# Attention and a bilinear feed-forward in one kernel: a fixed list in place of the scheduler

## The chip, the core and the metric

The kernel runs on one core of a Trainium2 chip. The metric is the device time of one execution in microseconds (us); the median of three runs before the change is 1517.46 us (1517.1 to 1517.92).

## The reference, cut to what matters

```python
# attention block: q, k, v are (8, 12, 448, 64), float32; g_q, g_k are (64,)
def rmsnorm(x, g):
    rms = np.sqrt(np.mean(x * x, axis=-1, keepdims=True) + 1e-06)
    return x / rms * g
q_n, k_n = (rmsnorm(q, g_q), rmsnorm(k, g_k))
scores = scale * np.matmul(q_n, k_n.transpose(0, 1, 3, 2))
attn = np.exp(scores - np.max(scores, axis=-1, keepdims=True))
attn = attn / (np.sum(attn, axis=-1, keepdims=True) + 1e-09)
attn_out = np.matmul(attn, v)
# feed-forward block: x is (3584, 768); w_a, w_b are (768, 1536), w_out is (1536, 768)
a = x @ w_a
b = x @ w_b
out = a * b @ w_out
```

The attention output of all 12 heads becomes the 3584 x 768 input of the feed-forward.

## The kernel before, in words

**The work.** The attention is done in 24 steps, one for each pair of head pairs (four heads of one batch); the code calls such a step `p`. For each step the SP queue loads q, k and v (L435). ScalarE squares q and k (L458), VectorE sums the squares (L460) and scales them (L464), GpSimd takes the power -0.5 (L466), VectorE multiplies q by it (L470). TensorE transposes k and then the scaled q (tile `pt`, L496), ScalarE copies both out of PSUM into `qkT` (L501, L503). Then seven blocks of keys follow, `j` = 0 to 6. For each, TensorE makes a scores group (`sc`, L517), ScalarE takes two exponentials of it (`ET`, L523), TensorE multiplies them by v (`o`, L539). The sums over keys are either four more matmuls for each block (`su`, L575, in the first five steps) or additions of the `ET` tiles on VectorE and GpSimd (L553) with one `su` group at the end. ScalarE moves the sums out (L588), they go to DRAM and back to be inverted in a compact form (L595, L608, L600, L604), ScalarE copies `o` out (L635) and VectorE multiplies it by the inverse (L646). The groups `sc`, `o` and `su` each consist of four 64 x 64 matmuls on the four quadrants of the array; the profile counts each as two passes, so such a group shows as 8 matmuls. All other matmuls use the full 128 x 128 array. The planner calls the two modes `quad` and `full`.

**The feed-forward** runs in four stages of two batches each, all with Strassen-like seven-product schemes: `firsts` makes a and b and their product, `lasts` multiplies it by w_out. In the first two stages the first product is L1202 (`pq`) and the last L903 (`po`); in the last two stages a deeper scheme is used (L779, `da` and `dg`, with VectorE's L818, L819, L826, L831 and L802), and L1100 for a part of the last product (`a`, `b`, `d`, `e`, `g`, with VectorE's sums `Si`, L1076). During the attention of the first two batches, ScalarE (L271) and VectorE (L272 to L280, L394) also turn the weights from the words they are given in into fp32 factors, 18 tiles `st`, which go to DRAM and come back when a stage needs them.

**PSUM.** Eight banks: the tag `sc` has two tiles of two banks each, and is used by the transposes, the scores, the sums and, later, by `dg`, `d` and `g`; the tag `o` has one tile of two banks; the tag `mm` has two tiles of one bank, used by `pq`, `po`, `da` and others.

**What sets the order.** Every operation is recorded by `Plan.op` (L49) with its engine, an estimated duration, a key (its due time), the operations that it depends on, the tiles that it opens, and a function that emits it. `Plan.run` (L72) then schedules them all: it walks through time, keeps for each engine the candidates whose inputs are ready, and takes for the engine that can start first the candidate with the lowest key among those that could start within 0.2 us (PE) or 0.05 us (others) of the earliest. It charges `TURN` for a change of the PE's mode, `STAY` to discourage leaving the quad mode, `LAG` for each step between engines, `RATE` and `LANDING` for DMAs. The functions are called in the order of time found, which is the program order on each engine and also the order in which tiles of a pool go round. Each engine works through its own instructions in that order.

Of the kernel before, what the change touches and what calls it, by code (L numbers as in the profile page):

```python
# [12 lines left out]
AF = mybir.ActivationFunctionType  # L13
ALU = mybir.AluOpType
# [10 lines left out]

class Plan:
# [9 lines left out]
    TURN = 0.18  # L36
    LANES = 8
    RATE, LANDING = 300.0, 2.0
    STAY = 0.3
    LAG = 0.1  # L40
# [31 lines left out]
    def run(self):  # L72
        ops = self.ops
        links, first = {}, {}
        for n, o in enumerate(ops):
            if o[6] is not None:
                links.setdefault(o[6], []).append(n)
        for c in links.values():
            for n in c:
                first[n] = c[0]  # L80
        users, need, left, last = {}, {}, {}, {}
        for n, o in enumerate(ops):
            head = first.get(n, n)
            outer = {d for d in o[4] if first.get(d, d) != head}
            need[head] = need.get(head, 0) + len(outer)
            for d in outer:
                users.setdefault(d, []).append(head)
            for t in o[9]:
                left[t] = left.get(t, 0) + 1
        ready = {n: 0.0 for n in need}  # L90
        opened, free, modes, cands, dma, port = {}, {}, {}, {}, 0.0, 0.0
        for n, k in need.items():
            if k == 0:
                cands.setdefault(ops[n][0], []).append(n)

        def members(n):
            return links[ops[n][6]] if ops[n][6] is not None else [n]

        def buffers(n):

            t, taken = 0.0, {}
            for x in members(n):
                for name in ops[x][8]:
                    tag, bufs = self.tags[name]
                    had = opened.setdefault(tag, [None] * bufs)
                    since = [(last.get(o, 0.0), k) for k, o in enumerate(had) if (tag, k) not in taken.values() and not left.get(o)]
                    if not since:
                        return None
                    t, taken[name] = max(t, min(since)[0]), (tag, min(since)[1])
            return t, taken  # L110

        order, end, sent = [], {}, [0.0] * self.LANES
        while any(cands.values()):
            best = None
            for e, cs in cands.items():
                f = free.get(e, 0.0) if e else 0.0
                at = {}
                for n in cs:
                    t = buffers(n)
                    if t is not None:  # L120
                        t = t[0]
                        turn = self.TURN if ops[n][5] != modes.get(e) else 0.0
                        if e == "PE" and modes.get(e) == "quad" and turn:
                            turn += self.STAY
                        at[n] = max(f, ready[n], t, port if ops[n][10] else 0.0,
                                    sent[ops[n][11] - 1 - self.LANES] if ops[n][11] else 0.0) + turn
                if at:
                    t = min(at.values()) + (0.2 if e == "PE" else 0.05)
                    n = min((n for n in at if at[n] <= t), key=lambda n: (ops[n][2], n))
                    t = at[n] - (self.STAY if e == "PE" and modes.get(e) == "quad" and ops[n][5] != "quad" else 0.0)  # L130
                    if best is None or t < best[0]:
                        best = t, e, n
            t, e, n = best
            cands[e].remove(n)
            for name, (tag, k) in buffers(n)[1].items():
                opened[tag][k] = name
            for x in members(n):
                if ops[x][5] != modes.get(e) and x != n:
                    t += self.TURN
                modes[e] = ops[x][5]  # L140
                order.append((t, x))
                t += ops[x][1]
                end[x] = t
                if ops[x][10]:
                    port = max(port, t)
                if ops[x][7]:

                    dma = max(dma, t) + ops[x][7] / self.RATE
                    end[x] = dma + self.LANDING
                    sent += [end[x]] * ops[x][11]  # L150
                for name in ops[x][9]:
                    left[name] -= 1
                    last[name] = max(last.get(name, 0.0), end[x])
                for u in users.get(x, ()):
                    ready[u] = max(ready[u], end[x] + (self.LAG if ops[u][0] != e else 0.0))
                    need[u] -= 1
                    if need[u] == 0:
                        cands.setdefault(ops[u][0], []).append(u)
            if e:
                free[e] = t  # L160
        assert len(order) == len(ops)
        self.times = order, end
        for _, n in order:
            if ops[n][3] is not None:
                ops[n][3]()


# [3 lines left out]
def kernel(  # L171
# [35 lines left out]
    nc = tc.nc  # L207
# [3 lines left out]
    P = 128  # L211
# [87 lines left out]
    def fast_body(ld, wk, ps_s, ps_o, ps_mm, dram):  # L299
# [27 lines left out]
        def rounding(key, size, get, x, w):  # L327

            for e, n, emit, r, wr in round_steps(get):
                rate = {"ACT": 950, "DVE": 1900 if n == 1 else 950, "POOL": 420}[e]  # L330
                names = {"x": x, "w": [w]}
                op(e, 0.17 + size / rate, key, emit, sum((names[c] for c in r), []), sum((names[c] for c in wr), []),
                   lock=e != "ACT")
# [25 lines left out]
        def factors(n, key, early, after):  # L359
# [16 lines left out]
            for part in range(2):  # L376
# [9 lines left out]
                op(LOADS, 0.45, key - 0.75, load, after, [f"{row}/{part}"], kb=768)  # L386
# [3 lines left out]
            for pool_, to, x, y in steps:  # L390
                add = to == 4 and not last
                e = FACTOR if pool_ else "DVE"
                op(e, 1.05 if e == "POOL" else 0.6, key,
                   lambda e=e, to=to, x=x, y=y, add=add: two[e].tensor_tensor(  # L394
                    sts[n][:, to], sts[n][:, x], sts[n][:, y], ALU.add if add else ALU.subtract),
                   [f"{st}/{homes[x]}", f"{st}/{homes[y]}"], [f"{st}/{homes[to]}"], lock=True)
# [11 lines left out]
        def stream(beta, n, f=None):  # L408
# [10 lines left out]
            op("SP", 0.5, 6.0 * beta + n / 4, load, reads, [f"{st}/{x}" for x in range(7)] + ["streaming"], new=[st],  # L419
# [6 lines left out]
        def loads(p, nm):  # L426
# [11 lines left out]
            op("SP", 0.8 if nm != "k" else 1.4, p - (1.8 if nm == "v" else 2.0), emit, [f"firsts{PREP}"] if p >= HELD else [], [t], new=[t],  # L438
               kb=460 if nm != "k" else 800, dmas=2)

        def normalize(p):
# [8 lines left out]
            def squares(s, nm):  # L450
# [8 lines left out]
                op("ACT", 1.07, key, square, [f"{nm}{p}"], [sq], new=[sq])  # L459
                op("DVE", 1.1, key, lambda: nc.vector.tensor_reduce(rs[p][:, s], xs["sq", nm, p], AX, ALU.add), [sq], [f"{ms}/{nm}"])  # L460

            def roots(a, b, names):
                msf = lambda: rs[p][:, a:b].rearrange("p s n -> p (s n)")
                op("DVE", 0.2, key, lambda: nc.vector.tensor_scalar(msf(), msf(), 1.0 / D, 1e-6, ALU.mult, ALU.add), [], names)  # L464
                op("POOL", 2.7 if b - a == 1 else 5.0, key,
# [20 lines left out]
        def transposes(p):  # L486

            qkT, key = tile_of(f"qkT{p}", "qkT", 2), p - EARLY
            for n, nm in ((1, "k"), (0, "q")):
# [17 lines left out]
                op("ACT", 1.05 if n else 1.15, key, take, [pt, "gain"], [f"{qkT}/{n}"], new=[qkT] if n else [])  # L507

        def scores(p, j):
# [17 lines left out]
            op("ACT", 1.12, p, exps, [sc, f"ms{p}/k"], [E], new=[E])  # L527
# [15 lines left out]
        def add_up(p, j):  # L543
# [10 lines left out]
            op(e, 2.2 if e == "POOL" else 1.12, p, emit, [f"E{p}.{j}"] + ([f"E{p}.0"] if j == 1 else []), [t],  # L554
# [24 lines left out]
        def invert(p):  # L579
# [27 lines left out]
            op("SP", 0.8, p - 0.0, spread_out, [t], [few], new=[few], kb=20, dmas=2)  # L607
            op("DVE", 0.3, p - 0.0, lambda: nc.vector.reciprocal(fews[0], fews[0]), [], [few])  # L608
            op("SP", 0.4, p - 0.0, leave, [few], [f"inv{p}"], kb=20)
            op("SP", 1.0, p - 0.0, come_back, [f"inv{p}"], [t], kb=460, dmas=2)  # L610
# [88 lines left out]
        def deep_factors(beta, m):  # L699
# [6 lines left out]
            for n, x, y, alu, reads in ((0, w(1, 0), w(1, 1), ALU.add, []), (1, made(0), w(0, 0), ALU.subtract, [0]),  # L706
# [9 lines left out]
                op("SP", 0.5, 0, lambda n=n: nc.sync.dma_start(kept["s"][:, m, :, n], ts[n]), [nm], [f"ks{m}.{n}"], kb=448)  # L716

        def deep_products(beta, key, names, h):
# [12 lines left out]
            for f, x in enumerate(xs_of):  # L731
# [4 lines left out]
                for n, a, b in ((0, lambda t=token: t(0, 1), lambda t=token: t(0, 0)), (1, lambda t=token: t(1, 1), lambda k=block: k(0)),  # L736
# [6 lines left out]
                    op("DVE", 0.32, -0.4, emit, [f"{x}/0", f"{x}/1", "ended" if beta == ONCE else f"{h}/open"] + ([nm] if n else []),  # L743
# [5 lines left out]
            def step(m, f, F, names_F):  # L749
# [10 lines left out]
                op("SP", 0.9, 6.0 * beta + (7 * m + f) / 14, load, [f"kept{2 * m}", f"kept{2 * m + 1}"] + [f"ks{m}.{n}" for n in range(5)],  # L760
# [10 lines left out]
                def product(nm, to, terms, reads, new=None, more=False):  # L771
# [9 lines left out]
                    op("PE", len(terms) * HS / 595, key + 0.1 * (7 * m + f), emit, reads + [slot], [nm, "ffn"],  # L781
# [19 lines left out]
                def wide(to, other):  # L801
                    take("DVE", 1.02, lambda: V.tensor_tensor(F[to], F[to], F[other], ALU.add), allF(other), allF(to), lock=True)  # L802

                def times(g, i, n):
                    e = "DVE" if m == MH - 1 and f > 4 else TIMES
                    take(e, 1.2 if e == "POOL" else 0.63,
# [19 lines left out]
                take("DVE", 0.66, lambda: V.tensor_tensor(  # L826
# [36 lines left out]
        def last_product(beta, h, key):  # L863
# [48 lines left out]
            def add(to, x, t, names_in, names_out):  # L912

                return lambda po, ps: op("DVE", 0.6, -1, lambda: nc.vector.tensor_tensor(to(), x(), ps(), ALU.add),
                                         [po] + names_in, names_out)

            def out_(t, i, x, y):
# [3 lines left out]
                def take(po, ps):  # L921
# [5 lines left out]
                    op("DVE", 0.6, -1, emit, [po, f"{fin}/{'cU'[y]}{t}"], [o_sb], new=[o_sb])  # L927
# [564 lines left out]
```

## Time and profile before

| what | value |
|---|---|
| median of three runs | 1517.46 us |
| the profiled execution | 1517.54 us |
| its span, first to last instruction | 1515.7 us |
| TensorE busy (7854 matmuls) | 1477.4 us, 97% of the span |
| VectorE busy | 1009.6 us, 67% |
| ScalarE busy | 441.2 us, 29% |
| GpSimd busy | 324.7 us, 21% |
| mean granted TensorE clock | 0.999 |
| moved by DMA | 250.73 MB, mean 165 GB/s |

The span is 1.84 us shorter than the execution's own time. The page gives busy time by engine, then the same in 40 slices of about 38 us, each digit in tenths. The waits view lists for each engine and line how long it stood still and what ended the wait. The timeline lists instructions in order, merged where they follow each other; an idle time ahead of one stands in brackets with what ended it. Ends of matmuls are modelled, so distances between the starts of matmuls are the safer measure; they are used here.

By what TensorE does, the span has these stages: attention alone with the making of the weights up to about 185 us, attention with `pq` to about 230 us, `pq` alone to 386 us, attention with `pq` and `po` to 540 us, `pq` alone to 731 us, attention with `po` to 920 us, and then feed-forward alone to the end.

### The profile page before, as it was taken

The numbers are of one execution on the slowest core, as the hardware profiler recorded it, in microseconds if no ns is written. First come the engines' busy times: TensorE is split into PE (matmuls) and PEld (weight loads), VectorE is DVE, ScalarE is ACT, GpSimd is POOL, SyncE is SP. The second block draws the span as 40 slices with busy tenths as digits, with TensorE's granted clock in tenths as the row PEclk, the third lists the DMA queues.
The fourth block names the chain that finished last, engine by engine and source line by source line (L and its number), as shares of the span: only waits on it lengthen the run. The fifth ranks groups of instructions, "written<-read, shape, count | busy, mean of one in ns | idle before, by whom it ended". The sixth has DMA issues, their size and how long they took to land.

```text
span 1515.7 us, 21017 instructions
## 1 busy us (share of the span) xinstructions
PE 1477.4 (97%) x7854; PEld 981.6 (65%) x7854; DVE 1009.6 (67%) x1568; ACT 441.2 (29%) x790; POOL 324.7 (21%) x172
## 2 busy tenths in 40 slices
PE   8998999999999999999999999999999999999998
PEld 5553345555445555555544445699997889999798
DVE  5887869888784233343667656477777667777785
ACT  6777661111554000000177761011111011111000
POOL 3426442111241001000265541011210001211000
PEclk9999999999999999999999999999999999999999
DMA  9897455554532464555656534655555755554554
GB/s 274 247 283 194 99 111 181 189 200 156 156 109 75 130 191 136 167 177 182 184 134 169 119 115 123 186 156 157 157 157 187 254 165 158 157 157 135 197 172 118
DMA packets 189074, 250.73 MB, mean 165 GB/s; under 512 B 61988, under 2 KB 160804, under 8 KB 182308
## 3 DMA queue, kind: packets, MB, share of 16 engines
q1 hardware_dynamic: 160900, 195.82, 45.5%
q10 hardware_dynamic: 28064, 53.48, 10.0%
q8 instruction: 64, 1.05, 0.3%
q14 instruction: 46, 0.38, 0.1%
HBM read 191.10 MB, written 57.97 MB: 164 GB/s over the span
## 4 chain that ended last, share of the span: by engine, by line
PE 86%; DMA 6%; DVE 3%; ACT 2%; issue 1%; SPq 1%; ACTq 0%; DVEq 0%
PE pq L1202 25%; PE dg L779 17%; PE po L903 15%; PE da L779 6%; PE o L539 6%; PE sc L517 6%; PE g L1100 2%; PE a L1100 2%; PE pt L496 2%; DMA q_sb<-in_q_dram 2%; PE su L575 1%; ACT ET L523 1%; PE b L1100 1%; DMA kept_o<-st 1%; PE d L1100 1%
## 5 line engine op out<-in xcount | busy, mean ns | idle before, releaser
L1202 PE MATMUL pq<-x,st 128*128 128x448 f32 x1008 | 382.4, 541 | 0.0
L1202 PEld LDWEIGHTS pq<-x,st 128*128 128x128 f32 x1008 | 190.8, 190 | 188.7 <-issue 181.7
L523 ACT ACTIVATE ET<-sc,ms 128x448 f32<-128x448 f32 x336 | 192.3, 632 | 86.5 <-PE sc L517 71.1
L539 PE MATMUL o<-ET,v_sb 64*64 64x448 f32 x1344 | 192.5, 546 | 3.6 <-ACT ET L523 2.9
L517 PE MATMUL sc<-qkT 64*64 64x448 f32 x1344 | 180.0, 543 | 16.3 <-ACT ET L523 9.1
L466 POOL TENSOR_TENSOR ms<-ms,expo 128x14 f32<-128x14 f32 x48 | 151.3, 3154 | 176.2 <-DVE ms L464 175.6
L779 PE MATMUL dg<-x,st 128*128 128x224 f32 x672 | 169.6, 355 | 2.0 <-DVE dF L826 2.0
L779 PE MATMUL dg<-dT,st 128*128 128x224 f32 x672 | 168.3, 353 | 1.9 <-DVE dt L819 1.9
L903 PE MATMUL po<-st,hT 128*128 128x384 f32 x492 | 163.4, 488 | 0.0
L807 POOL TENSOR_TENSOR hT<-dF 128x448 f32<-128x448 f32 x42 | 47.6, 1143 | 427.3 <-DVE dF L802 427.3
L903 PEld LDWEIGHTS po<-st,hT 128*128 128x128 f32 x492 | 92.9, 190 | 66.9 <-issue 6.0
L779 PEld LDWEIGHTS dg<-x,st 128*128 128x128 f32 x672 | 126.5, 190 | 5.3 <-DVE dF L826 5.3
L779 PEld LDWEIGHTS dg<-dT,st 128*128 128x128 f32 x672 | 126.7, 190 | 3.2 <-DVE dt L819 2.8
L779 PE MATMUL da<-x,st 128*128 128x224 f32 x504 | 123.2, 353 | 1.1 <-ACT dt L792 1.1
L517 PEld LDWEIGHTS sc<-qkT 64*64 64x64 f32 x1344 | 60.7, 133 | 89.6 <-issue 35.5
L539 PEld LDWEIGHTS o<-ET,v_sb 64*64 64x64 f32 x1344 | 61.3, 132 | 81.1 <-ACT ET L523 42.3
L553 POOL TENSOR_TENSOR sum<-sum,ET 128x896 f32<-128x896 f32 x38 | 81.1, 2134 | 104.0 <-ACT ET L523 60.8
L779 PEld LDWEIGHTS da<-x,st 128*128 128x128 f32 x504 | 93.0, 190 | 4.5 <-ACT dt L792 2.1
L802 DVE TENSOR_TENSOR dF<-dF 128x896 f32<-128x896 f32 x84 | 93.3, 1111 | 3.4 <-DVE dF L831 0.5
L792 ACT COPY dt<-da 128x224 f32<-128x224 f32 x84 | 29.1, 346 | 209.2 <-PE da L779 209.2
L553 DVE TENSOR_TENSOR sum<-sum,ET 128x896 f32<-128x896 f32 x57 | 62.0, 1088 | 38.2 <-POOL sum L553 34.0
L903 PE MATMUL po<-st,fin 128*128 128x384 f32 x252 | 86.7, 492 | 0.0
(136 smaller groups left out, 1683.6 us busy)
## 6 DMA issues: line engine op xcount, KB each, us to landing
st<-kept_o SPq DMA_DIRECT2D x28, 1152.0 KB
st<-kept_s SPq DMA_DIRECT2D x84, 320.0 KB
kept<-st ACTq DMA_DIRECT2D x12, 1344.0 KB
st<-kept SPq DMA_DIRECT2D x12, 1344.0 KB
st<-kept SPq DMA_DIRECT2D x84, 192.0 KB
ti<-kept_t SPq DMA_DIRECT2D x48, 288.0 KB
kept_s<-ds SPq DMA_DIRECT2D x30, 448.0 KB
q_sb<-in_q_dram SPq DMA_DIRECT2D x48, 224.0 KB
```

The lines of the kernel that those rows point to most:

```text
L466: lambda: nc.gpsimd.tensor_tensor(msf(), msf(), expo[:, 0:2 * NT * (b - a)], ALU.pow), [], names)
L496: nc.tensor.transpose(t[:, j * P:(j + 1) * P], x[:, j].rearrange("p h d -> p (h d)"), ident)
L517: nc.tensor.matmul(t[low_high[w], e, 0:S], lhsT=qkTs[p][low_high[e], 1, j * P + w * D:j * P + (w + 1) * D], rhs=qkTs[p][low_high[e], 0, w ...
L523: nc.scalar.activation(E[:, e], scs[p, j][:, e, 0:S], AF.Exp, scale=rs[p][:, 1, 2 * j + e:2 * j + e + 1])
L539: nc.tensor.matmul(os_[p][low_high[e], w, 0:S], lhsT=xs["v", p][low_high[w], e, j * D:(j + 1) * D], rhs=ETs[p, j][low_high[w], e], start=( ...
L553: two[e].tensor_tensor(sums[p], sums[p] if j > 1 else ETs[p, 0], ETs[p, j], ALU.add)
L779: nc.tensor.matmul(to(), lhsT=W(w), rhs=t(), start=not more and k == 0, stop=k == len(terms) - 1, skip_group_check=True)
L802: take("DVE", 1.02, lambda: V.tensor_tensor(F[to], F[to], F[other], ALU.add), allF(other), allF(to), lock=True)
L807: lambda: two[e].tensor_tensor(C(i, n), F[g][:, 0:S], F[g][:, S:2 * S], ALU.mult), allF(g),
L903: nc.tensor.matmul(held["po"][:, 0:HALF], lhsT=a[0]()[:, c], rhs=sts[beta, 12 + place_of[f]][:, c], start=(c == 0), stop=(c == MH - 1))
L1100: nc.tensor.matmul(held[bank], lhsT=x()[:, c], rhs=y(c), start=(start and c == 0), stop=(stop and c == MI - 1), skip_group_check=True)
L1202: nc.tensor.matmul(banks[bank][:, 0:S], lhsT=sts[at][:, f, c * P:(c + 1) * P], rhs=quads[x][:, c], start=(start and c == 0), stop=(stop an ...
```

## The change

The scheduler in `Plan.run` is taken out. In its place stands a list, compressed into a string, that gives for each place in time which operation comes there. Nothing is decided any more when the kernel is built: `run` walks through the list and calls each operation's function, and asserts that each one's inputs come ahead of it. The operations themselves, their tiles and pools stay. The estimated durations in many calls of `op`, and the constants of `Plan`, are changed too. The words that came with the change say that the list was found by a local search, in which two-bank PSUM tiles count as one and DMA issues are longer.

```diff
+ORDER = (
+    "c-rk(30PEDmj3U3?^P95ul9va1q8L*rPZ`%qMdZRqsBExlWsd|1d&n^aAjXy;t~+|4MYox8>keZqKJYT7c?p^Xtp-vBxZBc^UZWVrzc<cH|M<q"
...
+)
...
-    TURN = 0.18
+    TURN = 0.13
     LANES = 8
-    RATE, LANDING = 300.0, 2.0
+    RATE, LANDING = 310.0, 1.85
     STAY = 0.3
-    LAG = 0.1
+    LAG = 0.04
+    OVER = {"DVE": 0.085, "ACT": 0.1, "POOL": 0.04}
+    LATE = {"PE": 0.16}
...
     def run(self):
+
         ops = self.ops
-        links, first = {}, {}
...
-        self.times = order, end
-        for _, n in order:
-            if ops[n][3] is not None:
-                ops[n][3]()
+        n = len(ops)
+        places = zlib.decompress(base64.b85decode(ORDER))
+        assert len(places) == 2 * n
+        rest, at = list(range(n)), {}
+        for k in range(n):
+            x = rest.pop(places[k] + 256 * places[n + k])
+            assert all(d in at for d in ops[x][4])
+            at[x] = k
+            if ops[x][3] is not None:
+                ops[x][3]()
...
-            op("SP", 0.8 if nm != "k" else 1.4, p - (1.8 if nm == "v" else 2.0), emit, [f"firsts{PREP}"] if p >= HELD else [], [t], new=[t],
+            op("SP", 1.28 if nm != "k" else 1.4, p - (1.8 if nm == "v" else 2.0), emit, [f"firsts{PREP}"] if p >= HELD else [], [t], new=[t],
                kb=460 if nm != "k" else 800, dmas=2)
...
-            op("ACT", 1.12, p, exps, [sc, f"ms{p}/k"], [E], new=[E])
+            op("ACT", 1.15, p, exps, [sc, f"ms{p}/k"], [E], new=[E])
```

Some forty more calls of `op` differ in the same way, in the estimated duration alone.

## The prediction

> **What bounds the kernel now.** I read the page first, then the waits of TensorE, then TensorE's timeline around those waits, and last the busy time by stage.
>
> ```profile
> PE 1477.4 (97%) x7854; PEld 981.6 (65%) x7854; DVE 1009.6 (67%) x1568; ACT 441.2 (29%) x790; POOL 324.7 (21%) x172
> ...
> PE   8998999999999999999999999999999999999998
> ...
> PEclk9999999999999999999999999999999999999999
> DMA  9897455554532464555656534655555755554554
> ```
>
> TensorE (PE) is busy 97% of 1515.7 us at full clock, so an order can only win what PE loses between matmuls. Slices 1 to 6, 11 to 14 and 20 to 24 hold the attention. The DMA engines are nearly full only in the first three slices.
>
> ```profile
> PE sc L517 <- ACT ET L523: 9.1, 15, 1.5
> PE sc L517 <- ACT qkT L503: 6.1, 9, 1.2
> PE o L539 <- ACT ET L523: 2.9, 6, 0.8
> PE dg L779 <- DVE dF L826: 2.0, 2, 1.0
> PE dg L779 <- DVE dt L819: 1.9, 2, 1.0
> PE b L1100 <- DVE Si L1076: 1.8, 1, 1.8
> ```
>
> Columns: us in total, times, longest. Most named waits are attention groups that wait for ScalarE (ACT). Modelled ends hide part of each, so I go by starts:
>
> ```profile
> 139.39 0.98 PE L517 MATMUL sc<-qkT 64*64 64x448 f32 x8 [0.52 <-ACT ET L523]
> 140.19 0.93 PE L539 MATMUL o<-ET,v_sb 64*64 64x448 f32 x8
> 141.65 0.98 PE L517 MATMUL sc<-qkT 64*64 64x448 f32 x8 [0.52 <-ACT ET L523]
> ```
>
> Unhindered groups start 0.752 us apart (137.18 and 137.93 in the same view). Here scores and values take 2.26 us in place of 1.504, so 0.76 is lost each round, 0.05 of it on the restart. The reason: both rounds write the same PSUM pair, since the other one is held by a sums tile, so the scores wait for the exponentials of the scores just written, with one group as cover. That chain is 0.30 (hand-over) + 1.16 (two exponentials) = 1.46, less 0.752 of cover = 0.71, which the trace shows with the restart.
>
> ```profile
> 73.47 1.74 PE L517 MATMUL sc<-qkT 64*64 64x448 f32 x16 [1.14 <-ACT qkT L503]
> 75.58 1.12 PE L539 MATMUL o<-ET,v_sb 64*64 64x448 f32 x5 [0.37 <-ACT ET L523]
> ```
>
> The second kind: a new step's scores directly after its transposes wait for the copy of q (1.01 us on ACT and the hand-over), 1.21 us beyond the pace, and the first values then wait again. The third: at 1454 us `b` waits 1.97 us (start to start) because VectorE (DVE) has three other sums queued ahead of `Si`.
>
> By starts, PE loses 82 us in all against the pace of each kind of matmul: 7 in the first 25 us, 36 from 25 to 230, 6.5 from 386 to 540, 18 from 731 to 920, 14.5 after that. Of this, 52 quad stretches cost 0.11 at their end and 0.09 at their start each: 10.6 us.
>
> **What the Trainium skill says.** PSUM — Partial Sum Buffer, Engine vs sequencer instructions: the queues of ScalarE, VectorE and GpSimd are strict FIFO, and matmuls start and complete in program order. The trace agrees: at 1454 `Si` runs only after three 0.95 us sums that nothing hurries. So the order alone decides such stalls. TensorEngine Tiling (Array Packing), Key Properties: a change of tiling mode drains TensorE; here it costs 0.09 to 0.11 us. The same page, PSUM Bottleneck: tiling speeds up TensorE but not the emptying of PSUM; here a group of 0.752 faces 1.16 us of exponentials. Trainium Kernel Development and Optimization, Key Constraints: DMAs of SP, ACT and GpSimd share the same 16 engines; the DMA row at 9, 8, 9 shows how little is spare there.
>
> **The change part by part.** The new durations and constants do nothing by themselves: `run` no longer reads them. The built programs hold the same instructions on each engine, 4095 matmuls among them (fallback branch apart); only places and waits differ. So the whole effect is the order. It keeps the staging: the last matmul of each stage has the same work ahead of it within a few us, and the step between `pq` and `po` is unchanged. I counted, in both built orders, each PE wait for ACT or DVE whose chain goes back to an earlier matmul over at most four instructions, and set its length (traced durations; 0.30 hand-over for ACT; 0.2 for DVE, an estimate that gives the `dg` waits of 1.12 as 0.97) against the PE work between. Places with less cover than chain:
>
> - Scores into the pair just written (and a sums group after them): before 15 places of 0.71 = 10.6 us. After, five full ones (3.5) and eleven smaller ones (4.6), one of which waits behind the copy of `o`, = 8.1 us. The two-in-one-pair rounds at 110 to 150 us are still there, fewer.
> - Scores after the transposes: before 4 of 1.21 and 5 of 0.46 = 7.1 us. After 1 and 2 = 2.1 us, because other groups stand between.
> - Values after exponentials: before 7.1 us in 15 places, mostly 0.52 right behind the stalls above. After none.
> - Feed-forward alone: before `Si` 2.04, two `dg` of 0.97, two `da` of 0.65, one `b` of 0.33 = 5.6 us. After 3.2 us: three of the four `Si` are moved ahead of the three sums, one `dg` shrinks to 0.59.
>
> Before 30.4, after 13.4: **17.0 us gone**. As a check, the same count names in the order before the four stalls of 1.2 us and the rounds of 0.71 that the trace has. About 20 fewer restarts of 0.05: 1.0 us. Quad stretches fall from 52 to 48: 4 x 0.20 = 0.8 us.
>
> What is late next: about 9 us of PE stalls before have a longer chain, such as 1.3 us at 200 us, where ACT stands at a square that waits for its q load and everything behind it in ACT's queue waits too. Moved loads count here. By the waits, the PE work between the point that lets a q or k load go and its square is under 5 us for nine of 45 loads before and for one after (medians 6.0 and 8.7). Additions ahead of the `su` groups get more time too (least 3.0 before, 3.8 after). So these 9 us should rather shrink; bounds: 5 gained to 6 lost, I take 2 gained. PE has 57 more waits of its own (404 against 347): between nothing and 57 x 0.05 = 2.9 us, I take 1.3.
>
> SP's queue holds the same loads, stores and returns of the inverse, GpSimd's the same powers and sums, past each other by a few places; ACT's weight loads move likewise. Each would cost only where it makes a square, a copy or a sum late, which the 5 to 6 us of the bounds hold. Cover gone would be that of loads: a late load costs about 2 us (ACT's waits for q: 13.5 us, 8 times).
>
> Sum: 17.0 + 1.0 + 0.8 + 2 - 1.3 = 19.5 us. The profiled execution is 1517.54 (span 1515.7 + 1.84), so 1498.0; it stands 0.08 above the median, so the forecast is **1498 us**.
>
> **The rivals.**
> *The stalls move up the chain* (15%). ACT has 82 of 120 us busy from 110 to 230, DVE 90; if half of what is removed comes back as waits for loads, powers or additions, 9 to 10 us remain: 1508. For it: no stage alone is bound by PE here. Against: the cover of loads and sums is longer too.
> *Everything upstream goes as well* (13%): 17 + 1.8 + up to 9: about 1490. For it the longer covers; against it the DMA row.
> *The waits are exchanged one for one* (4%), because the count misses chains that are longer than four instructions: 1516 to 1519.
> *Late loads* (8%, slower). In the first 110 us DMA is 92% busy. If weights go out ahead of q and k so that each of 16 loads comes 2 us later than its cover, ACT's FIFO passes all of it on to PE: 32 - 19 = 13 us lost, 1531. It decides from about ten such loads. Against it: one load with short cover after, and the weights' work that must be done by each transpose stays within 8 us of what it was.
> *The list does not act*: excluded, since the built orders differ on every engine.
>
> **How the numbers follow.** The main case, 1494 to 1503, has 60%. With the 15% at 1508 and half of the 13%, the range 1489 to 1511 leaves out under 20%; its ends are the bounds above (5 more gained and no wait cost; 6 lost, 2.9 of waits and part of the count not won). A run of this kernel can tell about 0.2%, 3 us. Faster by more than that: 60 + 15 + 13 = 88%; within: 4%; slower: 8%.
>
> **What would show it.** Right: TensorE's idle time from 731 to 920 us nearly without ACT's exponentials; the waits for `qkT` down from 6.1 us in 9 places to about 2 in 3; no wait for `Si`; scores still waiting for exponentials around 110 to 150 us; the stages without attention as long as before. Wrong: more idle of ACT ahead of L458, or of PE behind loads, in the first 230 us.

## The result and the profile after

| | us |
|---|---|
| list, median of five runs | 1498.88 (1498.09 to 1502.80) |
| scheduler's order, run beside it, median of five | 1517.92 (1517.10 to 1519.69) |
| ratio | 0.9880, 95% interval 0.9864 to 0.9896 |
| profiled execution of the list, its span | 1502.80, 1500.9 |

The list is 19.0 us faster; the forecast was 1498 (1489 to 1511). The profiled execution is the slowest of its five, 3.9 us above the median. In its profile every line number is 34 lower than before: scores L483, exponentials L489, values L505, sums L541, copies of k and q L467 and L469, squares L424, weight loads L347 and L350.

The page, the same four rows as shown of before:

```profile
PE 1466.2 (98%) x7854; PEld 957.4 (64%) x7854; DVE 1003.3 (67%) x1568; ACT 438.8 (29%) x790; POOL 320.7 (21%) x172
...
PE   8988999999999999999999999999999999999998
...
PEclk9999999999999999999999999999999999999999
DMA  9888545555342455445667544655555765554554
```

The instruction counts are the same, so only places differ. In TensorE's first six slices one digit has fallen and none has risen: the start did not get better. The mean granted clock is 0.997, where it was 0.999. TensorE's waits (us in total, times, longest):

```profile
PE sc L483 <- ACT qkT L469: 6.9, 5, 3.7
PE sc L483 <- ACT ET L489: 6.8, 11, 0.9
...
PE o L505 <- ACT ET L489: 2.1, 3, 1.2
PE pt L462 <- ACT ET L489: 2.0, 2, 1.3
...
PE dg L745 <- DVE dF L792: 0.2, 1, 0.2
```

The exponentials ahead of scores fell from 9.1 us in 15 places to 6.8 in 11, and the wait for `Si` is gone. The copies of q did not fall to about 2 us: they are 6.9 us, 3.7 of them in one place. By starts, TensorE loses 67.3 us against the pace of its kinds of matmul where it lost 81.9. Of this the first 150 us take 37.0 (29.7 before), 150 to 230 us 7.5 (13.4), and all after that 22.8 (38.8). What the first 150 us of the list lose is in part matmuls at a lower clock, shown below.

A full stop of the first kind is still there. TensorE's timeline of the list:

```profile
153.84 0.93 PE L505 MATMUL o<-ET,v_sb 64*64 64x448 f32 x8
155.30 0.98 PE L483 MATMUL sc<-qkT 64*64 64x448 f32 x8 [0.53 <-ACT ET L489]
```

1.46 us lie between these starts in place of 0.752, the 0.71 of the forecast. In the attention with `po` such stops went. First the scheduler's order at the second scores of a step, then the list at that point of a later step:

```profile
791.22 0.98 PE L517 MATMUL sc<-qkT 64*64 64x448 f32 x8
792.02 0.93 PE L575 MATMUL su<-sum,ones 64*64 64x448 f32 x8
793.48 0.98 PE L517 MATMUL sc<-qkT 64*64 64x448 f32 x8 [0.53 <-ACT ET L523]
794.28 0.93 PE L539 MATMUL o<-ET,v_sb 64*64 64x448 f32 x8
```

```profile
893.47 0.93 PE L483 MATMUL sc<-qkT 64*64 64x448 f32 x8
894.22 0.93 PE L541 MATMUL su<-sum,ones 64*64 64x448 f32 x8
895.09 2.20 PE L869 MATMUL po<-st,fin 128*128 128x384 f32 x6
897.22 0.98 PE L483 MATMUL sc<-qkT 64*64 64x448 f32 x8
```

The list puts a product of w_out between the sums and the scores; it covers the exponentials.

**Where the time went, by place.** Both orders pass through places at which the same operations have been done, but for one at most, whatever their inner order: after 437, 1031, 1927, 2422 and 2786 operations, among others. The start of TensorE's first matmul after such a place can therefore be compared between runs (read from the traces):

| place | scheduler | list | what lies before it |
|---|---|---|---|
| 437 | 124.75 | 134.52 | attention with the making of weights |
| 1031 | 367.65 | 370.39 | the rest of it, attention with `pq`, `pq` alone |
| 1927 | 801.84 | 800.39 | attention with `pq` and `po`, `pq` alone, half a step with `po` |
| 2422 | 954.97 | 945.26 | attention with `po` |
| end of span | 1515.7 | 1500.9 | feed-forward alone |

The list loses 9.8 us by place 437 and wins all of its gain, and more, afterwards. The largest early stop, in the list's timeline of TensorE:

```profile
81.30 1.74 PE L483 MATMUL sc<-qkT 64*64 64x448 f32 x16 [3.74 <-ACT qkT L469]
```

And the chain of waits that leads to it (start, length, what; pieces under 0.3 us are left out):

```profile
65.08 6.15 DMA few<-rec
71.49 0.91 DVE st L238
72.42 0.97 DVE st L239
73.41 1.77 DVE st L241
75.20 0.97 DVE lraw L243
76.20 1.77 DVE lraw L244
77.99 1.77 DVE st L246
79.78 0.41 ACTq L350
80.23 1.02 ACT qkT L469
81.30 1.78 PE sc L483 x16
```

Read from the bottom: the scores wait for the copy of q; the copy stands on ScalarE behind a weight load (L350); the load waits until VectorE has rounded the words that its tile still holds; and VectorE began that late because it stood at the reciprocal of a step's sums (`few`, L574) until they had come back from DRAM.

A second early loss lies at the very start. Of the 40 warm-up matmuls (`warm`), which have no part in the result, the scheduler's order has 32 ahead of the first transposes of k and 8 behind them, the list 16 ahead, 16 behind and 8 after the first scores. First the scheduler's order, then the list:

```profile
8.17 0.96 PE L496 MATMUL pt<-ident,k_sb 128*128 128x128 f32 x7 [1.36 <-DMA k_sb<-in_k_dram]
9.36 1.16 PE L1293 MATMUL warm<-ident 128*128 128x128 f32 x8
```

```profile
7.93 1.73 PE L462 MATMUL pt<-ident,k_sb 128*128 128x128 f32 x7 [3.07 <-DMA k_sb<-in_k_dram]
10.10 3.79 PE L1259 MATMUL warm<-ident 128*128 128x128 f32 x16
```

The list's TensorE stands longer for k, and the granted clock is then below full: 0.83 from 0 to 12 us and 0.89 from 12 to 24, where it is 1.00 in the scheduler's order. Its warm-up matmuls start 0.21 us apart behind this wait, the scheduler's 0.11. The first scores come at 16.25 us in the list and at 13.98 in the scheduler's order.

### The profile page after: what moved, and what is told of

It is laid out like the page before. It is cut to its first block, busy times and chain, and to the rows that moved or that the text cites. A ratio compares the mean times of both kernels' runs of the same rounds, so it can differ in the third digit from the quotient of the medians.

```text
span 1500.9 us, 21032 instructions
## 1 busy us (share of the span) xinstructions
PE 1466.2 (98%) x7854; PEld 957.4 (64%) x7854; DVE 1003.3 (67%) x1568; ACT 438.8 (29%) x790; POOL 320.7 (21%) x172
## 4 chain that ended last, share of the span: by engine, by line
PE 87%; DMA 5%; DVE 4%; ACT 2%; SPq 1%; issue 1%; POOL 0%; ACTq 0%; DVEq 0%; POOLq 0%
PE pq L1168 25%; PE dg L745 17%; PE po L869 16%; PE da L745 6%; PE sc L483 6%; PE o L505 6%; PE g L1066 2%; PE a L1066 2%; PE pt L462 2%; DMA k_sb<-in_k_dram 1%; PE b L1066 1%; PE e L1066 1%; PE d L1066 1%; DMA few<-rec 1%; PE su L541 1%; ACT ET L489 1%
## 5 line engine op out<-in xcount | busy, mean ns | idle before, releaser
L489 ACT ACTIVATE ET<-sc,ms 128x448 f32<-128x448 f32 x336 | 190.8, 636 | 66.9 <-PE sc L483 52.6
L432 POOL TENSOR_TENSOR ms<-ms,expo 128x14 f32<-128x14 f32 x48 | 144.6, 3016 | 168.3 <-DVE ms L430 168.1
L483 PE MATMUL sc<-qkT 64*64 64x448 f32 x1344 | 154.7, 545 | 14.2 <-ACT qkT L469 6.9
L505 PE MATMUL o<-ET,v_sb 64*64 64x448 f32 x1344 | 150.4, 540 | 2.1 <-ACT ET L489 2.1
L483 PEld LDWEIGHTS sc<-qkT 64*64 64x64 f32 x1344 | 46.6, 132 | 99.5 <-ACT ET L489 40.4
L505 PEld LDWEIGHTS o<-ET,v_sb 64*64 64x64 f32 x1344 | 51.4, 133 | 75.8 <-issue 62.7
L1216 POOL TENSOR_TENSOR hT<-hT,t 128x448 f32<-128x448 f32 x12 | 14.4, 1200 | 325.1 <-DVE t L1214 325.1
```

What stands on the lines that cost most here:

```text
L432: lambda: nc.gpsimd.tensor_tensor(msf(), msf(), expo[:, 0:2 * NT * (b - a)], ALU.pow), [], names)
L483: nc.tensor.matmul(t[low_high[w], e, 0:S], lhsT=qkTs[p][low_high[e], 1, j * P + w * D:j * P + (w + 1) * D], rhs=qkTs[p][low_high[e], 0, w ...
L489: nc.scalar.activation(E[:, e], scs[p, j][:, e, 0:S], AF.Exp, scale=rs[p][:, 1, 2 * j + e:2 * j + e + 1])
L505: nc.tensor.matmul(os_[p][low_high[e], w, 0:S], lhsT=xs["v", p][low_high[w], e, j * D:(j + 1) * D], rhs=ETs[p, j][low_high[w], e], start=( ...
```

## The experiments

The theories are named in each expectation; from `e_few` on the letters A to D keep their meaning. Each run has its own executions of the scheduler's order beside it: 1518.83 us for the first four below, 1518.19 for `e_few`, `e_load`, `e_mend` and `s_si`, 1519.76 for `b_lite`, `a_lite` and `s_pair`, 1519.32 for `lite_two`. "Gains" are against those.

### Parts of the two orders put together

```diff
-order = the_list
+order = scheduler[:437] + [x for x in the_list if x not in scheduler[:437]]    # h437
+order = the_list[:437] + [x for x in scheduler if x not in the_list[:437]]     # r437
+order = scheduler[:1927] + the rest as in the list                             # h1927
+order = scheduler[:2786] + the rest as in the list                             # h2786
```

`h437`. 

> The first 437 operations (about 125 us; both orders have the same set of operations there) in the scheduler's order, the other 3930 in the list's order. Theory A (the two profiles are typical: the list loses 9.8 us up to this place and wins 24.4 us after it): about 1489 us, some 10 us below the list. Theory B (the count of short covers holds in every stretch, so the list wins 2.3 us here too, and the 9.8 us are an accident of one execution): about 1501 us.

`r437`. 

> The reverse: the first 437 operations in the list's order, the rest in the scheduler's. Theory A: about 1518 + 10 = 1528 us, slower than before. Theory B: about 1515.5 us.

`h1927`. 

> The scheduler's order up to operation 1927 (about 801 us), the list's after it. Theory A: the profiles put 13.2 us of the gain after this place (8.3 in the attention from 801 to 955 us, 4.9 in the feed-forward after it): about 1504.5 us. Theory B: the count has 4 rounds of 0.71, three smaller ones and four mode changes there and 2.4 us in the feed-forward, about 8 us: about 1510 us.

`h2786`. 

> The scheduler's order up to operation 2786 (about 1060 us, inside the first deep feed-forward), the list's after it. Theory A: the profiles put 4.8 us after this place (2.4 between 1143 and 1258 us, 2.7 in the last 110 us): about 1513 us. Theory B: the count has 2.4 us (the sums Si and one dg): about 1515.5 us.

| run | median us | ratio, interval |
|---|---|---|
| h437 | 1494.72 | 0.9836 (0.9820 to 0.9852) |
| r437 | 1524.51 | 1.0035 (1.0022 to 1.0047) |
| h1927 | 1506.09 | 0.9919 (0.9902 to 0.9935) |
| h2786 | 1514.39 | 0.9968 (0.9958 to 0.9978) |

The list's first 437 places do lose: the list alone is 4.2 us slower than h437, and r437 5.7 slower than the scheduler's order. The 9.8 us of the profiles was too much, since this part varies between executions: in six profiles with the scheduler's order place 437 was reached at 124.7 to 129.0 us, in two with the list's at 132.7 and 134.5. By differences of the medians, the rest of the list wins 24.1 us: 11.4 between places 437 and 1927, 8.3 from 1927 to 2786, 4.4 after that. Of the expectations, r437 and h1927 came out nearer to theory A, h437 and h2786 midway. h437 is faster than both kernels.

### Taking the early stops away one by one

`e_few`: the reciprocals of steps 1 to 3 later on VectorE.

```diff
 DVE  rounding of a weight tile (first parts)
-DVE  reciprocal of few, its DMA issue on SP      (step 1 shown; steps 2 and 3 alike)
 DVE  rounding, two or three more operations
+DVE  reciprocal of few, its DMA issue on SP
```

> The list with three places changed: the reciprocals of the inverse of steps 1 to 3 (VectorE, L574, and the DMA issue that follows each) stand behind one to four more VectorE operations, so that their input has come back from DRAM when VectorE gets to them. In the list VectorE stands at them for 3.03, 2.72 and 2.62 us (at 71.3, 94.9 and 119.5 us), in the scheduler's order for none of the three. Theory A (VectorE standing at a DMA's return is the root: it makes the rounding of the weights late, ScalarE's weight load stands behind that, and the copy of q behind the load): the stop of 3.92 us at 81.3 falls to about 0.9 and that of 1.82 us at 125.1 goes, 4.8 us in all: 1494.1 us. Theory B (the place of the load ahead of the copy of q is enough by itself): at most the 1.8 us at 125: 1497. Theory C (the early loss is the transfers', not the queues'): 1499, and the waits come back elsewhere.

`e_load`: the weight load behind the copy of q.

```diff
 ACT  copy of k, step 3 (L467)
-ACT  weight load (L350)
 ACT  copy of q, step 3 (L469)
+ACT  weight load (L350)
```

> The list with one operation moved by one place on ScalarE: the weight load that stood ahead of the fourth step's copy of q (L350 ahead of L469) stands behind it. Theory A and B: the stop of 3.92 us at 81.3 us goes, since ScalarE can copy q as soon as its transposes are there (75.3 us or so); what follows ScalarE's load then waits, but the scores have other work: 1495.0 us. VectorE's wait of 3.03 us at the reciprocal stays in the trace. Theory C: 1499, the same stop appears at the next operation of ScalarE.

`e_mend`: both, and the first 39 places of the scheduler.

```diff
-order = the_list
+order = scheduler[:39] + [x for x in list_with_both_edits if x not in scheduler[:39]]
```

> The list with its first 39 places in the scheduler's order (the transposes of q of the first step ahead of one more warm-up group), the three reciprocals later and the load behind the copy of q. Theory A: 2.1 (first 39 places) + 3.9 (81.3 us) + 1.8 (125.1 us) = 7.8 us below the list: 1491 us, and so a little below the version with the first 437 places of the scheduler (1494.7). Theory C: 1497, the first 39 places alone.

Measured: e_few 1502.61 us (1501.53 to 1504.98), e_load 1499.38 (1498.00 to 1501.52), e_mend 1504.75 (1501.08 to 1506.11), against 1498.88 for the list. Each edit did what it said in its place: place 249, just behind the stop at 81.3, came at 75.25, 75.81 and 74.47 us. But at place 437 the three stood at 133.18, 131.81 and 133.45, and nothing was won in the end. VectorE's waits in the first 136 us, the list first and then e_few:

```profile
DVE few L574 <- DMA few<-rec: 8.4, 3, 3.0
DVE x L612 <- DMA rec<-inv: 2.1, 2, 1.1
```

```profile
DVE x L612 <- DMA rec<-inv: 7.3, 3, 2.8
```

With its reciprocals later, VectorE no longer stands at them, but at the multiplication that needs the inverse back from DRAM. In e_few, TensorE and ScalarE then show:

```profile
90.16 2.52 PE L483 MATMUL sc<-qkT 64*64 64x448 f32 x12 [4.11 <-ACT ET L489]
```

```profile
88.11 0.95 ACT L424 ACTIVATE sq<-k_sb 128x896 f32<-128x896 f32 x1 [5.42 <-DMA few<-rec]
88.13 0.53 ACTq L368 DMA_DIRECT2D kept_o<-st  x1
88.96 2.19 ACT L489 ACTIVATE ET<-sc,ms 128x448 f32<-128x448 f32 x4
```

ScalarE stood at a square of k until a transfer had landed, and the exponentials stood behind it: 4.3 us by starts, as large as the stop that was taken away. The granted clock was below full here too, 0.72 from 84 to 96 us, and the three groups from 90.16 to 94.69 took 4.5 us where they need 2.3. In e_load the copy of q was early, and the exponentials behind the load took its place: that stop is 2.0 us at 80.8. So theory A fell as a statement of what the time depends on, though its chain is what the trace shows. Waits that come back elsewhere are what theory C expected; e_few and e_mend came out even above its 1499 and 1497. How much of their times is the lower clock's, no run separates (in e_mend it was 0.86 from 84 to 96 and from 105 to 117 us).

### With less to transfer

The DMA engines are 96% busy to place 437 in the scheduler's order and 91% in the list's (windows of 125 and 135 us). `b_lite` and `a_lite` take part of that away in the two orders.

```diff
-                        queue[LOADS].dma_start(to, moe_w_out[k * P:(k + 1) * P, :])
+                        queue[LOADS].dma_start(to[:, 0:NW // cut], moe_w_out[k * P:(k + 1) * P, 0:NW // cut])
...
-                    nc.sync.dma_start(x[low_high[w]], pair.rearrange("h (p j) d -> p j h d" if nm == "k" else
-                                                                     "h (p j) d -> p h (j d)", j=NT))
+                    nc.sync.dma_start(to, pair.rearrange("h (p j) d -> p h (j d)", j=NT))
```

`cut` is 1 for the first load into each tile and 2 after that; the loads of w_a and w_b are cut alike.

> The scheduler's order with less to transfer: every weight load after the first into each of its two tiles brings only half of its bytes (the other half of the tile keeps its old words), and k comes in packets of 1792 bytes in place of 256 (its elements then lie in another order in its tile). So the factors of the weights and the scores are not those of the reference; the instructions and their order on every engine stay. By the packet times before, this takes some 27 of the 120 us of transfer work off the first 437 places: 14 loads at 1.1 to 1.4 us each, and 9 us of k. Theory D (the first 437 places, 125 to 134 us, are set by the transfers, 91 to 96% busy there, in either order): place 437 comes 8 us or more earlier, and the whole takes 1507 to 1511 us. Theory A (single standing queues make the stops, the transfers are hidden): place 437 moves by less than 3 us: 1515 to 1518.

> The list with the same cut in its transfers as the run beside it (half of each weight load after the first into each tile, k in packets of 1792 bytes; results are not those of the reference). With full transfers the list reached place 437 from 3.7 to 9.8 us after the scheduler's order. Theory D: with the transfers out of the way the list's own stops count, which were counted as 2.3 us less than the scheduler's for these places: it reaches place 437 at most 2 us after the scheduler's order with the same cut, and the two differ by 22 us or more in all: 1484 to 1488. Theory A: VectorE and ScalarE still stand in the wrong places, the list stays 4 to 8 us behind at place 437, and the two differ by 15 to 19 us: about 1497.

Measured: b_lite 1516.63 us (ratio 0.9979, 0.9971 to 0.9988), a_lite 1493.24 (0.9822, 0.9804 to 0.9841). The cut is 17 to 21 us of transfer work, not 27: the shares fell to 83% of 124 us and 79% of 129 us. In b_lite place 437 came at 123.81, 0.9 us ahead of the earliest of the six profiles with full transfers and 5.2 ahead of the latest; the whole took 3.1 us less than the scheduler's order beside it. So theory D's 8 us fell: transfers may cost the scheduler's order some 3 us, but they do not set its start, busy as the engines are.

For the list place 437 came at 128.78, 3.9 and 5.7 us ahead of its two profiles with full transfers, and 5.0 behind b_lite, as theory A had it. But in all the two kernels differ by 23.4 us, as theory D had it: a_lite has made the 5.0 us good by place 1031 (361.87 against 364.48). With full transfers the list gained 19.0 us and h437 24.1. So with lighter transfers little of the early loss reaches the end: the list's order suffers more from them than the scheduler's. The cut also lightens every later load of k, so this is shown for the kernel as a whole, not for the first 437 places alone.

### Named stops without the transfers, and the price of a stop

`lite_two` is a_lite with the edits of e_mend, and with three products of w_out moved in a later stage.

```diff
 PE   sums of the step before (su)
-PE   product of w_out (po), six matmuls
 PE   scores into the pair just written (sc)
+PE   product of w_out (po), six matmuls
```

> The list with the cut in its transfers (half of each weight load after the first into each tile, k in packets of 1792 bytes; results are not those of the reference) and two changes in two stages, read apart by the places. First: the edits that, with full transfers, only exchanged one stop for another (first 39 places of the scheduler, three reciprocals later, the weight load behind the copy of q). With the cut alone the list reached place 437 at 128.8 us, the scheduler's order at 123.8. If the named queues are what is left of the list's early loss, place 437 comes at 123 to 125 us; if others take their place here too, at 127 to 129. Second, in the attention with po: three products of w_out (two of 1.94 us that covered the exponentials ahead of scores into the pair just written, at 862 and 897 us of the list, one that covered the copies of the sums at 847) stand behind these scores. By the prediction's price this stage grows from 144.87 us by 0.71 + 0.71 + 0.5 = 1.9 us; if such stops are worth nothing because others give the time back, by less than 0.5. In all: 1490.1 us if both hold, 1495.1 if only the price holds, 1493.2 if neither.

Measured: 1498.47 us (1497.30 to 1498.96), above all three expectations. Place 437 came at 126.20, between the two expectations for it and 2.6 us ahead of a_lite; that is one profile each, and profiles of one order differed by 4.3 us there, so the share of the named queues is not shown. Nothing of it is left at place 1031, which came at 362.40 where a_lite has 361.87. The attention with `po` took 147.41 us (939.34 less 791.93) where a_lite takes 144.87: 2.54 us against 1.9 expected. (The whole is 4.1 us slower than a_lite by the profiles: 1.0 up to place 1927, 2.5 here, 0.6 after.) TensorE's timeline at the two stops of the 0.71 kind; in this kernel scores are L489, exponentials L495 and sums L547:

```profile
851.45 0.93 PE L547 MATMUL su<-sum,ones 64*64 64x448 f32 x8
852.91 0.98 PE L489 MATMUL sc<-qkT 64*64 64x448 f32 x8 [0.53 <-ACT ET L495]
```

```profile
887.08 0.93 PE L547 MATMUL su<-sum,ones 64*64 64x448 f32 x8
889.01 0.98 PE L489 MATMUL sc<-qkT 64*64 64x448 f32 x8 [1.01 <-ACT ET L495]
```

By starts these are 1.46 and 1.93 us apart in place of 0.752: 0.71 and 1.18; the third, at the copies of the sums, 0.64. At 889 us the first exponentials had also waited 0.70 us for GpSimd's power, which the missing product no longer hid. So a stop put into the list costs its price, once or more, and nothing gave it back in this run.

### One move at a time in the scheduler's order

`s_si`: three sums `Si` ahead of three long sums.

```diff
+DVE  Si, Si, Si (0.55 us each)
 DVE  long sum (0.95 us)
 DVE  take of g
 DVE  long sum, long sum
-DVE  Si, Si, Si
```

> The scheduler's order with three places changed: three of the four sums Si at 1454 us stand ahead of the three long sums (0.95 us each on VectorE) that nothing hurries. If the order on VectorE alone makes the stop, its 2.0 us go and nothing comes back: 1515.9 us. If the long sums, 1.7 us later, make the next product's sums late, half or more comes back at 1456 to 1462 us: 1517 to 1518.

`s_pair`: four products of w_out ahead of the scores, the move that the list shows at 895 us.

```diff
 PE   sums of the step before (su)
+PE   product of w_out (po), six matmuls
 PE   scores into the pair just written (sc)
 PE   values (o)
-PE   product of w_out (po), six matmuls
```

> The scheduler's order with four operations moved: at 793, 812, 831 and 849 us the product of w_out (po, 1.94 us on TensorE) stands ahead of the scores that wait for the exponentials of the pair they write to, and no longer behind the values that follow them. The number of changes of tiling mode stays. If the price in the prediction holds (0.71 us for each such place, all of it gone when the cover is longer than the chain), 2.8 us go: 1515.0 us, and no scores wait for exponentials at these four places. If the sums' or the values' PSUM tile comes free too late for what is now earlier, half or more stays: 1516.5 or more.

Measured: s_si 1517.44 us (ratio 0.9997, 0.9986 to 1.0009), s_pair 1521.52 (1.0011, 1.0001 to 1.0021). In s_si the stop of 2.0 us went, and one of 0.9 us came five groups later:

```profile
1456.92 1.24 PE L1066 MATMUL g<-ti,fin 128*128 128x192 f32 x6 [0.84 <-DVE fin L1122]
```

Now the three long sums hold up VectorE's taking of `g`, whose PSUM tile is wanted. The stretch from `e` at 1447.75 to `g` at 1463.95 takes 16.20 us, and 17.37 in the scheduler's order (1449.17 to 1466.54): 1.2 of the 2.0 us are won there. The whole time cannot tell; its interval reaches from 2.1 us faster to 1.4 slower. In s_pair the four stops went; three of 0.77 us and, at the first place, one of 1.1 came within the next three groups. One of the three, TensorE and then ScalarE:

```profile
820.12 0.98 PE L483 MATMUL sc<-qkT 64*64 64x448 f32 x8 [0.59 <-ACT ET L489]
```

```profile
817.22 0.95 ACT L424 ACTIVATE sq<-k_sb 128x896 f32<-128x896 f32 x1 [1.21 <-DMA k_sb<-in_k_dram]
818.90 1.16 ACT L489 ACTIVATE ET<-sc,ms 128x448 f32<-128x448 f32 x2 [0.74 <-PE sc L483]
```

On ScalarE a square, late through its load of k, now stands ahead of the exponentials that the moved scores need. s_pair took 360.8 us from place 1500 to 2422; other runs with the scheduler's order there took 356.6 to 360.0, so the expected gain of 2.8 is excluded. By its interval the whole is 0.2 to 3.2 us slower; that this stage is the reason is not shown.

What differs in the list at this point is ScalarE. Its waits for loads, first in the scheduler's order from 735 to 930 us, then in the list from 730 to 915:

```profile
ACT sq L458 <- DMA k_sb<-in_k_dram: 3.7, 5, 1.9
ACT sq L458 <- DMA q_sb<-in_q_dram: 2.0, 3, 1.3
```

```profile
ACT sq L424 <- DMA k_sb<-in_k_dram: 1.4, 1, 1.4
ACT sq L424 <- DMA q_sb<-in_q_dram: 0.6, 1, 0.6
```

The list's 2.0 us all lie ahead of place 1927, and behind it none is left, where the scheduler's order has 3.5. In four other runs with the scheduler's order there these waits sum to 4.5 to 10.0 us; in h437 and a_lite with the list's to 1.1 and 1.2, none behind place 1927. The stage from place 1927 to 2422 took 144.86 to 144.88 us in seven runs with the list's order, and 152.5 to 155.3 in five with the scheduler's: 152.5 in s_si with 2.0 us of such waits inside the stage, 155.3 in r437 with 6.4. From these two I estimate 0.6 us for each us of waits, so that late loads are some 2 of the 8.3 us that the list wins here. No run changed the loads alone, so this share is argued, not shown.

## Why the prediction was right, and where not

**The total** was right by two errors of opposite sign. The count split at place 437 held 2.3 us of gain before it, which leaves some 17 of the 19.5 for what follows; measured by medians were 4.2 to 5.7 of loss and 24.1 of gain. That errors of some 7 us each cancel is luck.

**Less cover than chain, 17.0 us gone.** The mechanism was right. `lite_two` shows that such a stop costs its price in the list (2.54 us for 1.9), and the stops left where the count said: scores waiting for exponentials at 155.3 in the list, hardly any from 731 to 920 us (0.8 us in one place, from 3.4 in seven), no `Si`. But s_pair and s_si show that it isn't had in full move by move. In s_pair nothing was won, since the square on ScalarE stood in the way; in s_si 1.2 of 2.0 us were won in the stretch, since the taking of `g` then came late. In the list neither of these new stops shows.

**What is late next, 2 us gained (bounds 5 gained, 6 lost).** This is the term that failed. It was one net term for the whole kernel, and the two rivals about it were both true in part, in different stages. Up to place 437 stalls moved up the chain: 4.2 us lost by the medians of h437 and the list, 5.7 by r437 and the scheduler. The warm-up matmuls at the start, with 2.3 us of delay to the first scores, stood in no term. In the attention with `po` late loads went as well: ScalarE's waits for q and k, 5.7 us before, are 2.0, as the longer covers of loads (median 6.0 to 8.7 us) had promised; by the estimate above some 2 us. The sign that the prediction named for being wrong, more idle time of ScalarE ahead of its squares in the first 230 us, hardly showed: its waits for q and k there are 11.7 us against 10.9. The sentence that ACT's weight loads "move likewise" counted none of them singly; one, put ahead of a copy of q, made the stop of 3.9 us. The Trainium skill's sentence on it (PSUM — Partial Sum Buffer, Engine vs sequencer instructions: ScalarE's queue is strict FIFO) was quoted in the prediction for VectorE's sums; the trace shows that on ScalarE it holds for a DMA issue as well: its copy stood 5.67 us behind one.

**Scores after transposes, 7.1 to 2.1.** Wrong in the place it mattered: 6.9 us of waits for the copy of q remain, since the count looks back over four instructions of compute and not through a load.

**Values after exponentials, 7.1 to none.** Not quite: 2.1 us of waits in three places remain, all in the first 150 us (2.9 in six before).

**Feed-forward alone, 5.6 to 3.2.** Right in direction and too small: 4.4 us by h2786, where 2.4 were counted, together with whatever the waits there cost.

**Quad stretches** 52 to 48, as counted. **57 more waits, 1.3 us**: nothing here measures it by itself.

**Late loads, 1531** (8%): the stretch and ScalarE's queue were right, but what stood in that queue was a weight load and not late q and k, and the size was not right: the first 437 places became slower by 4 to 6 us, where 32 us were priced. The 92% given there for the first 110 us is the share from 25 to 110; from 0 to 110 it is 94%.

**What stays open.** The list's early loss isn't one queue's: where the named stops were taken away, others came. With lighter transfers the 5.0 us at place 437 are made good by place 1031, so the loss takes both, this order and the full transfers. Which of the places of VectorE's, ScalarE's and SP's queues in the first 437 would have to change together was not found. Nor was the share of the clock: its mean was 0.995 to 0.997 in the five executions of the list and 0.999 in four of the five of h437. On 1497 us a difference of 0.002 is, as an estimate, at most some 3 us, of the 4.2 between the two. Taking the scheduler's order in the first 437 places as a whole is worth 4.2 us and gives the fastest version with full transfers, 1494.72 us.

## What to carry to other kernels

Price the stages apart: one net term for "what is late next" hid a loss of 4 to 6 us in one stage and a gain in another. Count DMA issues in an engine's queue as places at which its compute can stand, and follow what such an issue waits for. And of a stop that one move takes away, ask for its successor among the next groups: none of the five kernels that took single stops away, with all transfers in place, is shown to be faster for it (s_si kept 1.2 of 2.0 us in its stretch), while stops that were put in cost their full price in their stage.

## What the runs showed of the hardware that was not expected

DMA engines that are busy do not have to be what binds. To place 437 they were 96% busy in the scheduler's order; with 17 us of their work taken away, that place came 0.9 us ahead of the earliest of six profiles and 5.2 ahead of the latest. The share itself goes past full: it is 1.09 from 12 to 24 us. The Trainium skill warns of it (Perfetto Trace Analysis, Identifying the Most-Contended Engine: with 16 engines, occupancy misleads), and this case agrees.

A granted clock below full can follow a wait early in the run. In the list it followed the wait of 3.07 us at 7.93, in e_few the one of 4.11 us at 90.16; behind the list's wait of 3.74 us at 81.30 it stayed at 1.00 (72 to 96 us), so not each such wait is followed by it. In b_lite TensorE waited 2.1 us for its transposes at 11.6; the mean clock from 12 to 24 us was 0.72, and the two scores groups at 13.70 and the values group at 16.74 took 3.04 and 1.50 us to the next start where they need 1.50 and 0.752. In the scheduler's order, with a wait of 1.48 us there, the clock stayed at 1.00. It cost b_lite about 3 us at that point, and nothing that is left at place 150 (47.35 against 47.42).
